# Blockwise causal attention and a max-out MoE layer on one core: transposed q and k copied out of PSUM earlier and in two parts, and the first batch reordered

## The chip, the cores and the metric

The kernel runs on one core of a Trainium2 chip. The metric is the device time in microseconds (us) of one execution. A single execution was also recorded by the hardware profiler; all lines of a profile come from that one.

## The reference

```python
# q, k, v: (8 batches, 8 heads, 576 rows, 64), fp32
scores = q @ k^T / 8
mask   = (row // 64) >= (column // 64)        # causal by blocks of 64
attn   = softmax(where(mask, scores, -1e9))
x      = (attn @ v), heads side by side       # (4608 tokens, 512)
# moe: w1, w2 (512, 1024), w_out (1024, 512)
out    = maximum(x @ w1, x @ w2) @ w_out      # (4608, 512) fp32
```

## The kernel before

Heads are handled in pairs, p = 0 to 31, four pairs to a batch; two pairs with their own q and k loads make a group, g = 0 to 15. The attention of a pair makes transposed scores: keys lie on the partitions, so that exp on ScalarE (ACT) gives a tile aT that TensorE can use as weights against v. The MoE layer works on tokens as they get done. One program order is written by hand for all engines (`manual_schedule`): every engine runs its own instructions in the order of the calls, and waits where a semaphore tells it to.

The steps of one group are these.

- `load_qk` (L111) loads q and k of four heads on the queue of SyncE (SP). With `gated` a small memset on GpSimd (POOL) goes ahead, so that the load starts no earlier than that memset. `load_v` (L131) and `load_w` (L142) load v and the MoE weights from POOL's own queue, and turn them into bf16 on the way.
- `cast` (L125) makes bf16 of q or k, in parts on the engines that it is given.
- `transposes` (L297) transposes q or k of both pairs of a group on TensorE into two PSUM tiles, and returns `copy_out`, which copies them to SBUF (qT, kT): the first by VectorE (DVE), the second mostly by ACT.
- Scores go to PSUM by `burst_p`, `burst_q1`, `burst_q2`, `burst_q3` in batch 0 (L360 to L370) and by `tile_0`, `tile_1`, `tile_2` later (L382 to L399); `exp` (L344) follows on ACT; `mask` (L349) then sets blocks of aT to zero, on POOL unless another engine is named.
- `pad_keys` (L327) copies a little of kT on POOL.
- `av` (L413) multiplies aT by v and normalises on DVE, in two calls for a pair: row tiles 0 and 1 (6 matmuls), then 2, 3 and 4 (24 matmuls). The late one needs all masks of the pair.
- `x_out` (L441) transposes the result to xT, by TensorE and two copies. After the second group of a batch it raises `done_tokens`: 256 after rows 0 to 255 of batch 0, then 576.

MoE matmuls fill TensorE in between. `plan` (L244) makes a list of units: `h_unit(i, f)` is x @ w1 and x @ w2 for a span i of tokens and 128 columns f (8 matmuls), `y_unit` multiplies by w_out. Span 0 is tokens 0 to 255, span 1 tokens 256 to 575, the others have 512 tokens. `fill(n)` (L281) issues steps of that list in order until their cost reaches n, and stops at the first step whose tokens are not done:

```python
    def fill(n):
        while n > 0 and at[0] < len(steps) and steps[at[0]][1] <= done_tokens[0]:
```

A matmul of span 0 costs 0.5, one of 512 tokens costs 1. `fill_of` (L467) gives each group's share of the steps that are ready.

PSUM has two pools: ps_s, two tiles of two banks, for scores; ps_m, four tiles of one bank, for everything else: the transposes, ps_h and ps_y of the MoE layer, ps_o of `av`, the tiles of `x_out`, and those of `warm_up` (L289), which are matmuls on zeros whose result is not used. A tile of ps_m can be taken again when its last reader is done.

Batch 0 (groups 0 and 1) is written out call by call, L501 to L580. The loop at L589 handles groups 2 to 15: scores of a pair, a `fill`, `av` of the pair two before, transposes of the next group (`t_pair`, L496), scores of the next tiles with their exps (`region`, L409), then `copy_out`, then POOL's work (`pool_work`, L474).

Of the kernel before, what the change touches and what calls it, by code (L numbers as in the profile page):

```python
# [9 lines left out]
BF16 = mybir.dt.bfloat16  # L10
# [4 lines left out]
def kernel(  # L15
# [10 lines left out]
    nc = tc.nc  # L26

    B, H, S, D = q.shape
    P = 128
# [6 lines left out]
    NFF = d_ff // P  # L36
# [6 lines left out]
    NP = 64  # L43
    RPP = S // NP
# [9 lines left out]
    NCH = 5  # L54
# [3 lines left out]
    QCUT = 256  # L58
# [14 lines left out]
    NSPAN = len(spans)  # L73
# [3 lines left out]
    tiles = [(carry[i] + w) // P for i, (_, w) in enumerate(spans)]  # L77
# [6 lines left out]
    qkn = ctx.enter_context(tc.tile_pool(name="qkn", bufs=2))  # L84
# [22 lines left out]
    raws = {}  # L107
    qk_n = {}
    dve, pool, act = nc.vector.tensor_copy, nc.gpsimd.tensor_copy, nc.scalar.copy

    def load_qk(g, queues, gated=False):  # L111
        b, u = divmod(g, GPB)
        for nm, src, queue in (("q", q, queues[0]), ("k", k, queues[1])):
            if queue is None:
                continue
            raws[nm, g] = t = raw.tile([P, 2, RPP * D], FP32, name=f"{nm}raw")
            if gated:
                nc.gpsimd.memset(t[:, 0, :1], 0.0)
            queue.dma_start(
                out=t[:],  # L120
                in_=src[b, 4 * u:4 * u + 4].rearrange(
                    "(s h) (p t) d -> (h p) s (t d)", h=2, t=RPP),
            )

    def cast(nm, g, parts):  # L125
        t = raws.pop((nm, g)).rearrange("p s (t d) -> p t s d", d=D)
        qk_n[nm, g] = n = qkn.tile([P, RPP, 2, D], BF16, name=f"{nm}n")
        for copy, j0, j1 in parts:
            copy(out=n[:, j0:j1], in_=t[:, j0:j1])  # L129

# [11 lines left out]
    def load_w(f0, fw, which=(0, 1)):  # L142
        for i in which:
            dst, src = ((w1_sb, w1r), (w2_sb, w2r))[i]
            nc.gpsimd.dma_start(out=dst[:, :, f0:f0 + fw], in_=src[:, :, f0:f0 + fw])
# [11 lines left out]
    nc.vector.memset(zeros[:], 0.0)  # L157
    nc.scalar.activation(out=warm[:], in_=warm[:], func=AF.Exp)
    load_qk(1, (SP, SP))
    load_qk(2, (SP, None))  # L160
    make_identity(nc, ident)
    for r in range(NV):
        nc.vector.memset(vv_r[r][:, :, :, D:D + 1], 1.0)
# [7 lines left out]
    for c in range(2):  # L171
        load_v(0, c)
    load_w(0, 256, (0,))
    cast("k", 1, ((pool, 0, RPP),))
    load_w(0, 256, (1,))
    load_qk(2, (None, SP), gated=True)


    done_tokens = [0]
# [64 lines left out]
    def plan():  # L244
        def h(i, f):
            t0, w = spans[i]
            units.append((h_unit(i, f), t0 + w, w / SPAN, 2 * NDM))

        def y(i, s, last=False):
            t0, w = spans[i]  # L250
            if last:
                units.append((y_last(i, s), t0 + w, 0.333, 3 * NFF))
            else:
                units.append((y_unit(i, s), t0 + w, 1.0, NFF))

        for i in range(NSPAN):
            for f in range(NFF):
                h(i, f)
                if i > 2 and f % 2 == 0 and f // 2 < tiles[i - 1]:
                    y(i - 1, f // 2)  # L260
            if i == 1:
                for j in range(2):
                    for s in range(tiles[j]):
                        y(j, s)
        n = tiles[-1]
        for s in range(n):
            y(NSPAN - 1, s, s == n - 1)
# [13 lines left out]
    def fill(n):  # L281
        while n > 0 and at[0] < len(steps) and steps[at[0]][1] <= done_tokens[0]:
            u, _, cost = steps[at[0]]
            next(u)
            n -= cost
            at[0] += 1


    def warm_up(n):  # L289
        pw = ps_m.tile([P, SPAN], FP32, name="ps_w", tag="m")  # L290
        for _ in range(n):
            nc.tensor.matmul(pw[:], zeros[:, :P], zeros[:], start=True, stop=True)
# [4 lines left out]
    def transposes(nm, g, copies):  # L297
        n = qk_n.pop((nm, g))
        pts = [ps_m.tile([P, RPP, NP], BF16, name=f"ps_{nm}T", tag="m") for _ in range(2)]
        for j in range(RPP):  # L300
            for i in range(2):
                r = slice(i * NP, (i + 1) * NP)
                nc.tensor.transpose(  # L303
                    pts[i][:, j, :], n[r, j].rearrange("p s d -> p (s d)"), ident[r, r],
                )

        def copy_out(which=(0, 1)):
            for i in which:
                t = (qT_r if nm == "q" else kT_r)[(2 * g + i) % NT]
                copies[i](  # L310
                    out=t[:, :S].rearrange("q (p j) -> q p j", j=RPP),
                    in_=pts[i].rearrange("q j p -> q p j"),
                )
        return copy_out

# [44 lines left out]
    def burst_p(p):  # L360
        burst(p, ((0, 0, QCUT), (1, P, QCUT - P)), 0)

    def burst_q1(p):
        burst(p, ((0, QCUT, 320), (1, QCUT, 192)), 384)

    def burst_q2(p):
        burst(p, ((1, 448, P), (2, QCUT, 320), (4, 512, BLK)), 896)
# [4 lines left out]
    def masks_p(p, eng=None):  # L372
        for a in (0, 256):
            mask(p, a, eng)

    def masks_q(p, eng=None):
        for a in (1024, 1408):
            mask(p, a, eng)
# [30 lines left out]
    def region(*tiles):  # L409
        for out in tiles:  # L410
            out()
# [26 lines left out]
            rec[:, :n].to_broadcast([P, n, 2, D]),  # L438
        )

    def x_out(g, t0=0, t1=NCH):  # L441
        b, u = divmod(g, GPB)
        xp = xps[g]
        n = t1 - t0
        n_odd = min(t1, NCH - 1) - t0
        pe = ps_m.tile([P, 2, n, BLK], BF16, name="ps_xe", tag="m")
        po = ps_m.tile([P, 2, n_odd, BLK], BF16, name="ps_xo", tag="m")
        for s in range(2):
            for t in range(t0, t1):
                src = xp[:, t, s].rearrange("p a d -> p (a d)")  # L450
                nc.tensor.transpose(pe[:, s, t - t0, :], src[:BLK], ident[:BLK, :BLK])  # L451
                if t < NCH - 1:
                    nc.tensor.transpose(po[:, s, t - t0, :], src[BLK:], ident[BLK:, BLK:])  # L453
        dst = xT[:, 2 * u:2 * u + 2, b * S + t0 * P:b * S + t1 * P].rearrange(
            "p s (t h w) -> p s t h w", h=2, w=BLK)
        nc.vector.tensor_copy(out=dst[:, :, :, 0], in_=pe[:])  # L456
        nc.vector.tensor_copy(out=dst[:, :, :n_odd, 1], in_=po[:])
        if u == GPB - 1:
            done_tokens[0] = min(b * S + t1 * P, (b + 1) * S)

# [37 lines left out]
        return lambda: [f() for f in outs]  # L498


    warm_up(16)  # L501
    cq = transposes("q", 0, (dve, act))
    ck = transposes("k", 0, (act, dve))
    cq((0,))
    ck((0,))
    cq((1,))
    ck((1,))
    cast("q", 1, ((dve, 0, RPP),))
    burst_p(0)
    masks_p(0)  # L510
    burst_p(1)
    warm_up(2)
    masks_p(1)
    for c in range(2, NCH):
        load_v(0, c)
    load_w(256, 256)
    cq = transposes("q", 1, (dve, dve))
    burst_q1(0)
    ck = transposes("k", 1, (dve, dve))
    for i in range(2):  # L520
        cq((i,))
        ck((i,))
    load_w(512, 512)
    warm_up(3)
    burst_p(2)
    av(0, [0, 1])
    burst_q3(0)
    warm_up(2)
    burst_p(3)
    masks_p(2, nc.vector)  # L530
    av(1, [0, 1])
    masks_p(3, nc.vector)
    burst_q2(0)
    av(2, [0, 1])
    warm_up(2)
    burst_q1(1)
    av(3, [0, 1])
    x_out(0, 0, 2)
    warm_up(2)
    cast("q", 2, ((pool, 0, RPP),))  # L540
    masks_q(0)
    cast("k", 2, ((pool, 0, RPP),))
    burst_q2(1)
    x_out(1, 0, 2)
    warm_up(2)
    burst_q3(1)
    masks_q(1)
    for c in range(3):
        load_v(1, c)
    fill(2)  # L550
    load_qk(3, (SP, SP), gated=True)
    burst_q1(2)
    transposes("q", 2, (dve, act))()
    fill(3)
    burst_q2(2)
    av(0, [2, 3, 4])
# [5 lines left out]
    av(1, [2, 3, 4])  # L562
    fill(2)
    burst_q1(3)
    transposes("k", 2, (dve, act))()
    pad_keys(4)
    pad_keys(5)
    fill(2)
    x_out(0, 2, NCH)
    burst_q2(3)  # L570
    av(2, [2, 3, 4])
    fill(2)
    burst_q3(3)
# [15 lines left out]
    for g in range(GPB, NG):  # L589
        a, b = 2 * g, 2 * g + 1  # L590
        if x_due:
            x_out(x_due.pop())
        n = fill_of(g)
        region(tile_0(a), tile_1(a))
        if g == GPB:
            av(3, [2, 3, 4])
            fill(5)
            x_out(1, 2, NCH)
            n = fill_of(g)
        lo, hi = n // 18, n * 2 // 9  # L600
        for p, tiles in ((a, lambda: (tile_2(a), tile_0(b))), (b, lambda: (tile_1(b), tile_2(b)))):
            fill(hi)
            if g > GPB:
                av_with(p - LAG, lo)
            else:
                fill(lo)
            copy_out = t_pair(p)
            region(*tiles())
            copy_out()
            if p % 2 and g + 1 < NG:  # L610
                pad_keys(p + 1)
                pad_keys(p + 2)
            pool_work(p)
        if g > GPB:
            x_due.append(g - 1)
        fill(n - 2 * (lo + hi))
# [43 lines left out]
```

The softmax here doesn't subtract the row's maximum and nothing guards it: scores larger than these inputs give would overflow.

## Time and profile before

| | us |
|---|---|
| median of 7 runs | 286.73 |
| lowest and highest | 286.25 and 288.73 |
| the profiled execution | 288.19 |
| its span, first to last instruction | 286.3 |
| ACT busy (exps of 128x1024: 92 of 1.02) | 140.9 |
| TensorE: ps_h, 412 matmuls of 128x512 | 102.4 |
| TensorE: ps_y, 273 matmuls | 65.5 |
| first ps_h matmul starts at | 18.23 |

A line of a timeline gives the start, the duration, the engine, the line of the kernel, the operation, out<-in with shapes, and how many instructions are put together; in brackets the engine's idle time just before, and what ended it. PE is TensorE, PEld its weight loads, SPq and POOLq the queues that issue DMAs. The rows of digits cut the span into 40 slices, with the busy share of each in tenths (for DMA, the mean of 16 DMA engines).

### The profile page before, as it was taken

The page shows a single profiled execution, that of the slowest core. Times are in us where ns is not written, and L with a number is a line of the kernel's source. Part 1 is how long each engine was busy: PE and PEld are TensorE (multiplying, and loading weights), DVE is VectorE, ACT ScalarE, POOL GpSimd, SP SyncE. Part 2 cuts the span into 40 slices and gives each one's busy share as a digit, 9 for nine tenths or more (in the row PEclk, how much of TensorE's full clock was granted, in tenths as well). Part 3 has the DMA queues.
Part 4 walks back from the last instruction along what each step waited for, and adds up shares of the span by engine and source line. Part 5 has one row for each costly group of instructions (what it writes and reads, how often), then busy time and mean ns, then how long its engine had stood idle before and what let it go on. Part 6 is the DMA issues. An engine that isn't in the chain of part 4 may idle for free.

```text
span 286.3 us, 7763 instructions
## 1 busy us (share of the span) xinstructions
PE 271.7 (95%) x3207; PEld 152.1 (53%) x3253; DVE 186.6 (65%) x386; ACT 140.9 (49%) x194; POOL 108.8 (38%) x271
## 2 busy tenths in 40 slices
PE   7689999999999999999999999999999999999995
PEld 2346667646555555555546464645555554444443
DVE  4966778758888676666667666667665766455430
ACT  2776486676575557383746646556555100010112
POOL 2987365754744643346253714362211000000000
DMA  7999989968954792669562985266210102011114
GB/s 258 264 208 201 194 200 283 228 86 255 212 35 167 83 231 49 204 71 228 61 205 35 201 93 164 78 76 73 49 39 37 39 37 76 37 64 50 56 54 147
DMA packets 55939, 36.67 MB, mean 128 GB/s; under 512 B 38752, under 2 KB 43232, under 8 KB 55904
## 3 DMA queue, kind: packets, MB, share of 16 engines
q0 software_dynamic: 41728, 7.87, 34.1%
q1 hardware_dynamic: 13760, 27.66, 28.4%
q10 hardware_dynamic: 416, 0.66, 0.7%
q8 instruction: 25, 0.41, 0.6%
q14 instruction: 10, 0.08, 0.1%
HBM read 34.60 MB, written 9.44 MB: 154 GB/s over the span
## 4 chain that ended last, share of the span: by engine, by line
PE 80%; issue 2%; ACT 2%; DVE 1%; ACTq 0%
PE ps_h L197 39%; PE ps_y L215 21%; PE ps_o L429 9%; PE ps_s L321 6%; PE ps_qT L303 2%; PE ps_kT L303 2%; PE ps_xe L451 2%; ACT aT L345 1%; DVE g L206 1%; PE ps_y L231 1%; PE ps_s L339 1%; ACT qT L310 0%; ACT aT L401 0%; ACT kT L310 0%; PE ps_xo L453 0%
## 5 line engine op out<-in xcount | busy, mean ns | idle before, releaser
L197 PE MATMUL ps_h<-xT,w_sb 128*128 128x512 bf16 (+3 forms) x604 | 133.9, 357 | 5.0 <-issue 3.2
L345 ACT ACTIVATE aT<-ps_s 128x1024 bf16<-128x1024 f32 (+2 forms) x100 | 95.9, 993 | 63.6 <-PE ps_s L321 51.8
L197 PEld LDWEIGHTS <-w_sb 128*128 128x128 bf16 x640 | 57.3, 98 | 58.5 <-issue 8.4
L204 DVE CAST h<-ps_h 128x512 bf16<-128x512 f32 (+3 forms) x80 | 51.0, 638 | 29.4 <-PE ps_h L197 27.7
L215 PE MATMUL ps_y<-wo_sb,g 128*128 128x512 bf16 x273 | 65.5, 379 | 0.8 <-issue 0.5
L206 DVE TENSOR_TENSOR g<-h,ps_h 128x512 bf16<-128x512 bf16 (+3 forms) x80 | 50.7, 634 | 11.7 <-PE ps_h L197 9.6
L350 POOL MEMSET aT<- 64x128 bf16 x124 | 22.4, 200 | 91.7 <-ACT aT L345 90.8
L221 ACT COPY y<-ps_y 128x512 f32<-128x512 f32 x31 | 18.3, 591 | 71.4 <-PE ps_y L215 56.7
L429 PEld LDWEIGHTS <-aT 128*128 128x128 bf16 x960 | 37.1, 98 | 15.7 <-issue 4.5
L215 PEld LDWEIGHTS <-g 128*128 128x128 bf16 x280 | 27.0, 98 | 32.1 <-issue 1.1
L429 PE MATMUL ps_o<-vv,aT 128*128 128x65 bf16 x960 | 40.2, 194 | 1.0 <-DMA vv<-in_v_dram 0.4
L133 POOL DMA_DIRECT2D vv<-in_v_dram x40 | 33.7, 847 | 0.5
L436 DVE TENSOR_TENSOR xp<-ps_o,rec 128x256 bf16<-128x256 f32 (+1 forms) x64 | 31.4, 491 | 2.2
L321 PE MATMUL ps_s<-qT,kT 64*128 64x64 bf16 (+6 forms) x344 | 31.8, 279 | 1.1 <-ACT kT L310 0.7
L435 DVE RECIPROCAL rec<-ps_o 128x4 f32<-128x4 f32 (+1 forms) x64 | 12.0, 187 | 24.5 <-PE ps_o L429 22.9
L129 POOL CAST qn<-qraw 128x1152 bf16<-128x1152 f32 (+1 forms) x15 | 16.5, 1100 | 8.8 <-DMA qraw<-in_q_dram 8.7
L187 POOL COPY g<-g 128x512 bf16<-128x512 bf16 x8 | 4.9, 614 | 38.5 <-DVE g L206 38.4
L129 POOL CAST kn<-kraw 128x1152 bf16<-128x1152 f32 x15 | 17.3, 1154 | 5.7 <-DMA kraw<-in_k_dram 5.7
L456 DVE COPY xT<-ps_xe 128x640 bf16<-128x640 bf16 (+2 forms) x18 | 8.2, 453 | 15.6 <-PE ps_xe L451 14.9
L321 PEld LDWEIGHTS <-kT 64*128 64x128 bf16 x344 | 13.7, 95 | 6.3 <-issue 2.8
L310 DVE COPY qT<-ps_qT 128x576 bf16<-128x576 bf16 x17 | 12.7, 749 | 0.7 <-PE ps_qT L303 0.7
L310 DVE COPY kT<-ps_kT 128x576 bf16<-128x576 bf16 x17 | 12.7, 749 | 0.4 <-PE ps_kT L303 0.4
(44 smaller groups left out, 141.6 us busy)
## 6 DMA issues: line engine op xcount, KB each, us to landing
qraw<-in_q_dram SPq DMA_DIRECT2D x16, 576.0 KB, 4.2
out_dram<-y SPq DMA_DIRECT2D x35, 256.0 KB, 2.6
kraw<-in_k_dram SPq DMA_DIRECT2D x15, 576.0 KB, 5.9
vv<-in_v_dram POOLq DMA_DIRECT2D x32, 128.0 KB, 5.3
w_sb<-in_moe_w_dram POOLq DMA_DIRECT2D x4, 256.0 KB, 8.7
w_sb<-in_moe_w_dram POOLq DMA_DIRECT2D x2, 512.0 KB, 12.5
wo_sb<-in_moe_w_out_dram POOLq DMA_DIRECT2D x2, 512.0 KB, 12.5
kraw<-in_k_dram ACTq DMA_DIRECT2D x1, 576.0 KB, 5.9
```

Of the source, the lines that this page charges most:

```text
L129: copy(out=n[:, j0:j1], in_=t[:, j0:j1])
L133: nc.gpsimd.dma_start(out=vv_r[b % NV][P - rows:, c, :, :D], in_=v[b, :, c * P:c * P + rows, :].rearrange("h p d -> p h d"),)
L197: nc.tensor.matmul(pt[:, :w], w_sb[:, c, f * P:(f + 1) * P], xT[:, c, t0:t0 + w], start=(c == 0), stop=(c == NDM - 1),)
L204: nc.vector.tensor_copy(out=h1[:, :w], in_=pt[:, :w])
L206: nc.vector.tensor_max(g[:, f, m:m + w], h1[:, :w], pt[:, :w])
L215: nc.tensor.matmul(py[:], g[:, f, s * P:(s + 1) * P], wo_sb[:, f, :], start=(f == 0), stop=(f == NFF - 1),)
L310: copies[i](out=t[:, :S].rearrange("q (p j) -> q p j", j=RPP), in_=pts[i].rearrange("q j p -> q p j"),)
L321: nc.tensor.matmul(ps[:, hh, col:col + w], kT[r, k0:k0 + P], qT[r, q0:q0 + w], start=True, stop=True,)
L345: nc.scalar.activation(out=aT_r[p % NA][:, :, a0:a0 + w], in_=ps[:, :, :w], func=AF.Exp, scale=scale,)
L350: (eng or nc.gpsimd).memset(aT_r[p % NA][BLK:, :, a0:a0 + BLK], 0.0)
L429: nc.tensor.matmul(po[:, gi, hh, :], a[:, hh, a0:a0 + P], vv[:, c, h0 + 2 * hh, :], start=(mm == 0), stop=(mm == n_mm - 1),)
L436: nc.vector.tensor_mul(xp[:, ts[0]:ts[0] + n, :, p % 2], po[:, :, :, :D], rec[:, :n].to_broadcast([P, n, 2, D]),)
```

## The change

The change has two parts.

The first is in the loop of groups 2 to 15 and touches every group: `copy_out()` is called ahead of `region(...)`, so the copies of qT or kT stand ahead of the exps in ACT's queue; and `lo`, the cost of MoE matmuls between the two `av` calls of a pair, is at least 3.

The second is batch 0. `copy_out` can copy a part of the columns, LOW (columns 0 to 260) or HIGH (261 to 575), and on a named engine. The copies of groups 0 and 1 are made in these parts. The casts of group 1 are shared by DVE and POOL. q and k of group 2 are both loaded later, gated behind the v loads of batch 0. All first halves of `av` and both `x_out` of rows 0 to 255 come before most of the bursts q1, q2 and q3; x_out of group 0 is copied by ACT. There are fewer warm-up matmuls (24 in place of 29). The transposes of group 2 come later, and `plan` orders the units of spans 0 and 1 by halves of f: f 0 to 3 of span 0, then of span 1, then f 4 to 7 of both.

```diff
     def cast(nm, g, parts):
-        t = raws.pop((nm, g)).rearrange("p s (t d) -> p t s d", d=D)
-        qk_n[nm, g] = n = qkn.tile([P, RPP, 2, D], BF16, name=f"{nm}n")
+        t = raws[nm, g].rearrange("p s (t d) -> p t s d", d=D)
+        if (nm, g) not in qk_n:
+            qk_n[nm, g] = qkn.tile([P, RPP, 2, D], BF16, name=f"{nm}n")
+        n = qk_n[nm, g]
...
     load_qk(1, (SP, SP))
-    load_qk(2, (SP, None))
...
     load_w(0, 256, (0,))
-    cast("k", 1, ((pool, 0, RPP),))
+    cast("q", 1, ((pool, 6, RPP),))
+    cast("k", 1, ((pool, 4, RPP),))
     load_w(0, 256, (1,))
-    load_qk(2, (None, SP), gated=True)
...
-        for i in range(NSPAN):
-            for f in range(NFF):
+        for f0 in (0, NFF // 2):
+            for i in range(2):
+                for f in range(f0, f0 + NFF // 2):
+                    h(i, f)
+        for i in range(1, NSPAN):
+            for f in range(NFF if i > 1 else 0):
                 h(i, f)
...
-        def copy_out(which=(0, 1)):
+        def copy_out(which=(0, 1), part=(0, NP), copy=None):
+            p0, p1 = part
             for i in which:
                 t = (qT_r if nm == "q" else kT_r)[(2 * g + i) % NT]
-                copies[i](
-                    out=t[:, :S].rearrange("q (p j) -> q p j", j=RPP),
-                    in_=pts[i].rearrange("q j p -> q p j"),
+                (copy or copies[i])(
+                    out=t[:, p0 * RPP:p1 * RPP].rearrange("q (p j) -> q p j", j=RPP),
+                    in_=pts[i][:, :, p0:p1].rearrange("q j p -> q p j"),
...
-    def x_out(g, t0=0, t1=NCH):
+    def x_out(g, t0=0, t1=NCH, copies=(dve, dve)):
...
+    LOW = (0, -(-QCUT // RPP))
+    HIGH = (LOW[1], NP)
     warm_up(16)
     cq = transposes("q", 0, (dve, act))
     ck = transposes("k", 0, (act, dve))
-    cq((0,))
-    ck((0,))
-    cq((1,))
-    ck((1,))
-    cast("q", 1, ((dve, 0, RPP),))
+    cq((0,), LOW)
+    ck((0,), LOW)
+    ck((1,), LOW)
+    cq((1,), LOW)
+    cq((0,), HIGH)
+    cast("q", 1, ((dve, 0, 6),))
+    cast("k", 1, ((dve, 0, 4),))
     burst_p(0)
     masks_p(0)
+    cq((1,), HIGH)
+    ck((0,), HIGH)
     burst_p(1)
+    ck((1,), HIGH)
     warm_up(2)
     masks_p(1)
+    load_w(256, 256)
     for c in range(2, NCH):
         load_v(0, c)
-    load_w(256, 256)
-    cq = transposes("q", 1, (dve, dve))
...
+    load_qk(2, (SP, SP), gated=True)
+    load_w(512, 512)
+    cq = transposes("q", 1, (dve, act))
+    ck = transposes("k", 1, (dve, dve))
+    cq((0,), LOW)
+    cq((1,), LOW)
+    ck((0,), LOW)
+    ck((1,), LOW)
+    cq((0,), HIGH, act)
+    cq((1,), HIGH, dve)
+    warm_up(2)
+    burst_p(2)
+    ck((0,), HIGH, act)
+    av(0, [0, 1])
+    masks_p(2, nc.vector)
+    burst_p(3)
+    av(1, [0, 1])
+    ck((1,), HIGH, act)
+    masks_p(3, nc.vector)
+    warm_up(1)
+    av(2, [0, 1])
+    x_out(0, 0, 2, (act, act))
+    warm_up(1)
+    av(3, [0, 1])
     burst_q1(0)
...
+    warm_up(1)
+    x_out(1, 0, 2, (dve, dve))
+    burst_q2(0)
+    warm_up(1)
+    fill(2)
     burst_q3(0)
...
+    masks_q(0)
     burst_q1(1)
...
+    fill(1)
     burst_q2(1)
...
+    fill(1)
     burst_q3(1)
     masks_q(1)
+    cast("q", 2, ((pool, 0, RPP),))
+    cast("k", 2, ((pool, 0, RPP),))
     for c in range(3):
         load_v(1, c)
     fill(2)
     load_qk(3, (SP, SP), gated=True)
     burst_q1(2)
-    transposes("q", 2, (dve, act))()
...
     burst_q1(3)
+    transposes("q", 2, (dve, act))()
+    fill(2)
+    x_out(0, 2, NCH)
+    burst_q2(3)
     transposes("k", 2, (dve, act))()
     pad_keys(4)
     pad_keys(5)
-    fill(2)
-    x_out(0, 2, NCH)
-    burst_q2(3)
     av(2, [2, 3, 4])
...
-        lo, hi = n // 18, n * 2 // 9
+        lo, hi = max(3, n // 18), n * 2 // 9
...
             copy_out = t_pair(p)
-            region(*tiles())
+            outs = tiles()
             copy_out()
+            region(*outs)
```

In the lines before, batch 0 ran its bursts q1, q3, q2 of pair 0 and q1 of pair 1 among the AVs of pairs 0 to 3, with `warm_up` calls of 2 and 3 between them.

More of the change, by code (lines that the diff above doesn't have):

```diff
@@ L455, in x_out @@
             "p s (t h w) -> p s t h w", h=2, w=BLK)
-        nc.vector.tensor_copy(out=dst[:, :, :, 0], in_=pe[:])
-        nc.vector.tensor_copy(out=dst[:, :, :n_odd, 1], in_=po[:])
+        copies[0](out=dst[:, :, :, 0], in_=pe[:])
+        copies[1](out=dst[:, :, :n_odd, 1], in_=po[:])
         if u == GPB - 1:
@@ L503 @@
     ck = transposes("k", 0, (act, dve))
-    cq((0,))
-    ck((0,))
-    cq((1,))
-    ck((1,))
-    cast("q", 1, ((dve, 0, RPP),))
+    cq((0,), LOW)
[5 more added lines that the diff above has]
+    cast("k", 1, ((dve, 0, 4),))
     burst_p(0)
     masks_p(0)
+    cq((1,), HIGH)
+    ck((0,), HIGH)
     burst_p(1)
+    ck((1,), HIGH)
     warm_up(2)
     masks_p(1)
+    load_w(256, 256)
     for c in range(2, NCH):
         load_v(0, c)
-    load_w(256, 256)
-    cq = transposes("q", 1, (dve, dve))
-    burst_q1(0)
[L519 to L526, printed above, removed]
-    burst_q3(0)
[L528 to L535, printed above, removed]
-    burst_q1(1)
[L537 to L542, printed above, removed]
+    load_qk(2, (SP, SP), gated=True)
[22 more added lines that the diff above has]
+    av(3, [0, 1])
+    burst_q1(0)
+    warm_up(1)
[3 more added lines that the diff above has]
+    fill(2)
+    burst_q3(0)
+    masks_q(0)
+    burst_q1(1)
+    fill(1)
     burst_q2(1)
-    x_out(1, 0, 2)
-    warm_up(2)
+    fill(1)
     burst_q3(1)
     masks_q(1)
+    cast("q", 2, ((pool, 0, RPP),))
+    cast("k", 2, ((pool, 0, RPP),))
     for c in range(3):
```

## The prediction

> **What bounds the kernel now.** I read the page's parts 1, 2 and 4, then the windows by stage, then each engine's timeline where TensorE isn't full.
>
> ```profile
> PE 271.7 (95%) x3207; PEld 152.1 (53%) x3253; DVE 186.6 (65%) x386; ACT 140.9 (49%) x194; POOL 108.8 (38%) x271
> PE   7689999999999999999999999999999999999995
> DMA  7999989968954792669562985266210102011114
> PE 80%; issue 2%; ACT 2%; DVE 1%; ACTq 0%
> ```
>
> TensorE is the bound: 95% busy and 80% of the chain. Only the first slices (7.2 us each) leave room, and there the DMA engines are full too. Work on TensorE isn't changed, warm-ups apart, so the end moves by what TensorE idles less or more. Two places matter.
>
> First, from 38 us to 210 us, TensorE waits a little for PSUM buffers which the copies of qT and kT still hold:
>
> ```profile
> 122.83 1.02 ACT L345 ACTIVATE aT<-ps_s 128x1024 bf16<-128x1024 f32 x1
> 123.75 0.63 ACT L310 COPY qT<-ps_qT 128x576 bf16<-128x576 bf16 x1
> ...
> 123.86 0.59 PE L197 MATMUL ps_h<-xT,w_sb 128*128 128x512 bf16 x2
> 124.43 0.65 PE L429 MATMUL ps_o<-vv,aT 128*128 128x65 bf16 x16
> ...
> 58.18 0.42 PE L303 MATMUL ps_kT<-ident,kn 64*128 64x64 bf16 x17 [0.40 <-ACT qT L310]
> ```
>
> The two ps_h matmuls issue 0.216 us apart, so ps_o could start at 124.29; it starts at 124.43, right after ACT's copy ends (123.75 + 0.63 = 124.38). That copy stood behind two exps.
>
> Second, batch 0. What sets its pace is GpSimd's queue and the loads:
>
> ```profile
> 11.62 0.37 SPq L119 DMA_DIRECT2D kraw<-in_k_dram  x1
> 24.26 0.37 SPq L119 DMA_DIRECT2D qraw<-in_q_dram  x1
> 24.67 0.47 SPq L119 DMA_DIRECT2D kraw<-in_k_dram  x1
> ...
> 19.95 1.15 POOL L129 CAST kn<-kraw 128x1152 bf16<-128x1152 f32 x1 [0.71 <-DMA kraw<-in_k_dram]
> 21.45 2.64 POOL L133 DMA_DIRECT2D vv<-in_v_dram  x3
> 24.33 0.34 POOL L350 MEMSET aT<- 64x128 bf16 x2
> 24.62 1.56 POOL L133 DMA_DIRECT2D vv<-in_v_dram  x2
> 31.43 1.15 POOL L129 CAST qn<-qraw 128x1152 bf16<-128x1152 f32 x1 [2.52 <-DMA qraw<-in_q_dram]
> 34.76 1.15 POOL L129 CAST kn<-kraw 128x1152 bf16<-128x1152 f32 x1 [2.18 <-DMA kraw<-in_k_dram]
> ...
> 22.18 0.78 PE L429 MATMUL ps_o<-vv,aT 128*128 128x65 bf16 x15 [0.44 <-DMA vv<-in_v_dram]
> 29.36 0.92 PE L429 MATMUL ps_o<-vv,aT 128*128 128x65 bf16 x24
> 31.98 1.48 PE L197 MATMUL ps_h<-xT,w_sb 128*128 128x256 bf16 x12
> ```
>
> A cast that ends its wait on a load shows the landing: k of group 2 took 8.3 us (11.62 to 19.95), q and k of group 3 7.2 and 10.1 us (24.26 to 31.43, 24.67 to 34.76). The v loads of batch 1 and the masks of pair 2 (24.33) stand behind the cast of k2. The late AV of pair 3 (29.36) comes 0.45 us after its masks end (28.71 + 0.20).
>
> **What the Trainium skill says.** "PSUM — Partial Sum Buffer", section "Engine vs sequencer instructions": the queues of ScalarE, VectorE and GpSimdE are strict FIFO. The trace agrees: the copy at 123.75 waits out the exps although its transposes were done at 121. "DMA: Bandwidth & Descriptors", section "Queues, rings and completion order": each DMA engine takes turns between the queues packet by packet, so a q load shares the engines with v and weights. The trace fits: 7.2 and 10.1 us to landing above, against 3.7 us at the fastest (listing of line 119). "TensorE: Matmul & The Clock Gate", Part 1: after an idle window of about 3.4 us the array runs at half clock. Before, the clock stays at 1.00 in every window; my gaps below stay under 2 us, so I cost this at nothing.
>
> **Part 1: copies ahead of the exps, and `lo` at least 3.** No instruction is added. ACT's copy moves before two exps; ACT is idle there (2.58 us until the exp at 121.48), so the exps end as late as before. Waits of TensorE that such copies end: 0.14 in each of the eight groups from 94 to 200 us (1.1), 0.40 at 58.18, about 0.3 each at 47.27 and 39.94: 2.1 us. Next late would be VectorE's release of a ps_h buffer; at 124.43 that had ended at 122.91. `lo` of 3 puts one more matmul (0.216 us) between two AV groups; five AV starts between 64 and 90 us wait 0.2 to 0.3 us for VectorE, 1.3 us together, and may lose all or none. Gain 0.8 to 3.2 us; I take 1.5, since a removed wait here often meets the next in a queue of four buffers.
>
> **Part 2: batch 0, edit by edit.** Copies: a 576-column copy (DVE 0.75, ACT 0.64) becomes 261 + 315 columns. From the ACT rows (128x384 exp 0.49, 128x1024 1.02: 0.83 ns a column, 0.16 fixed) the halves cost 0.37 + 0.42; on DVE about 0.42 + 0.48. The first exp can start at 9.0 instead of 9.29. But ACT now also has four HIGH copies before and between the exps of pairs 0 to 3 (1.7 us) and x_out(0)'s two copies (0.7). Group 1's casts: DVE 1280 columns (0.90 + 0.60) instead of 1152 (1.34), GpSimd 1024 (0.5 + 0.7) instead of 1152 (1.15): transposes of k1 0.2 us earlier at most, since they wait for the HIGH copies to free PSUM (10.5). Warm-ups: 24 instead of 29 matmuls, all in gaps: nothing.
>
> Followed along the queues: exps of pairs 2 and 3 at 12.9 and 14.0 (before 12.98 and 14.45), x_out(1) at 16.7, first ps_h at 17.6 (18.23 before): 0.6 earlier. The price is that the exps of q1 and q2 of pair 0 and q1 of pair 1, done by 17.2 before, now begin at 16.4. Then ACT runs on end: q1 of pair 2 at 20.9 (19.20 before), q1 of pair 3 at about 25.8.
>
> Loads: q2 and k2 leave at 15.8 (after w(256), v of batch 0 and two gate memsets on POOL) instead of 2.26 and 11.62. v of batch 0 is issued at 13.2 instead of 12.22, behind two more weight loads on POOL; it needed until 22.18 before, now 22.5 to 23.5. At 7.2 and about 9 us, q2 lands at 23 and k2 at 25 (23 to 26.5).
>
> POOL then, in order: cast k2 to 26.15, v(1) x3 to 28.75, gates 0.15, masks of pair 2 to 29.2, v(1) x2 to 30.8, pad_keys (0.3 each) to 31.4, masks of pair 3 to 31.8. Behind them on TensorE: late AV of pair 2 at 29.2 (before 26.61), of pair 3 at 31.85 (29.36). Then 0.85 us of AV, 0.8 of reciprocal and multiply, x_out, 0.7 of copies: ps_h resumes at 34.6, where 31.98 stood.
>
> Filler: the new order lets only f 0 to 3 of span 0 run before x_out(1): 4 units x 8 x 0.5 = 16 of cost. fill calls up to AV of pair 2 ask for 16, so fill(3) and fill(5) after it are empty, where the old order used 20. That is 8 matmuls x 0.109 = 0.87 us done later. Loss: 34.6 - 31.98 + 0.87 = 3.5 us, less 0.4 for the wait on the k3 cast at 35.97, which the later TensorE no longer meets: 3.1 us. A wait for a weight load (0.24 at 31.16, w of f 4) is inside the 31.98.
>
> **Sum.** +3.1 - 1.5 = +1.6 us. The profiled execution took 288.19 us with a span of 286.3, 1.9 outside it, and lies above the median of 286.73; I add the difference to the median: 288.3.
>
> **Rivals.**
> 1. The loads are not late (ends faster). Two loads less at the start; if k2 lands within 6.5 us of issue (by 22.5), its cast hides behind ACT's backlog, masks of pair 2 are done at 26.7, AV of pair 3 at 30.0, ps_h at 32.8 at the latest and 31.8 if v comes by 22. Loss 0.9; with the 2.3 of part 1: 285.3. For it: 3.7 us is the fastest landing. Against: both neighbours in that stretch took 7 us and more, with DMA at 9 tenths. It decides at k2's landing.
> 2. Both cancel: k2 at 24, part 1 at 2.2: +2.3 - 2.2, 286.8.
> 3. Batch 0 worse: ACT, with 2.4 us more in front of it, and v of batch 0 after 24 push one another, k2 at 26.5: ps_h at 36.5, loss 5, gain 1.5: 290.2.
> That the copies don't go ahead can't be: the calls are in that order on every queue.
>
> **Chances.** Forecast 0.43, rival 3 0.13, rival 2 0.26, rival 1 0.18. Half a per cent, 1.43 us, is what a measurement here can tell. Slower 0.55 (forecast's lower edge goes to "same"), within 0.27, faster 0.18. Range: rival 1 to a little beyond rival 3, 285.2 to 290.8; the forecast's own is 287.4 to 289.4.
>
> **What would show it.** Part 1: no gap before ps_o after qT copies, 58.18's wait gone. Part 2: k2's cast at 24 to 26 on POOL; masks of pairs 2 and 3 at 29 and 32; ps_o of pair 3 released by POOL; TensorE slices 4 and 5 emptier. Wrong if k2 is cast by 22.5, if ps_h runs on between 30 and 33, or if TensorE's clock falls below 1.00.

## The result: slower, and the profile after

| | before | changed |
|---|---|---|
| median of all runs, us | 286.93 (31 runs) | 291.00 (12 runs) |
| lowest and highest | 286.14 and 291.32 | 288.63 and 293.85 |
| the profiled execution, its span | 288.19, 286.3 | 291.21, 289.4 |
| `x_out(1, 2, NCH)`, the last of batch 0, starts on TensorE | 31.70 | 37.76 |
| first ps_y matmul | 50.97 | 56.91 |

Changed over before is 1.0119, with a 95% interval of 1.0096 to 1.0143: 3.4 us slower by the ratio, 4.1 by the medians.

The page of the changed kernel, parts 1, 2 and 4:

```profile
PE 272.4 (94%) x3205; PEld 153.0 (53%) x3248; DVE 184.4 (64%) x387; ACT 141.9 (49%) x202; POOL 108.2 (37%) x273
PE   8796689999999999999999999999999999999995
PEclk9999599999999999999999999999999999999999
DMA  7999979997993398529853893566211102011114
PE 86%; DMA 6%; POOL 5%; issue 2%; DVE 1%; ACT 0%; SPq 0%; POOLq 0%
```

In the second row TensorE's fourth and fifth slices (21.7 to 36.2 us) fell from 9 and 9 tenths to 6 and 6, and the granted clock (PEclk, in tenths of full speed) shows a 5 in the fifth. DMA and POOL have come into the chain, together 11%. From the seventh slice on the row is as full as before: the loss arises before 43 us.

SP's queue and GpSimd's timeline of the changed kernel:

```profile
15.79 0.37 SPq L119 DMA_DIRECT2D qraw<-in_q_dram  x1
16.20 0.98 SPq L119 DMA_DIRECT2D kraw<-in_k_dram  x1
```

```profile
24.80 1.14 POOL L131 CAST qn<-qraw 128x1152 bf16<-128x1152 f32 x1 [4.16 <-PE ps_h L198]
27.83 1.15 POOL L131 CAST kn<-kraw 128x1152 bf16<-128x1152 f32 x1 [1.88 <-DMA kraw<-in_k_dram]
28.92 2.63 POOL L135 DMA_DIRECT2D vv<-in_v_dram  x3
...
31.75 0.34 POOL L357 MEMSET aT<- 64x128 bf16 x2
...
34.23 0.20 POOL L357 MEMSET aT<- 64x128 bf16 x1
35.12 0.20 POOL L357 MEMSET aT<- 64x128 bf16 x1 [0.69 <-ACT aT L352]
```

The loads left when predicted, 15.8 and 16.2, and took 9.0 and 11.6 us until their casts could start. The releaser shown at 24.80, a ps_h matmul, can't be what a cast of q waits for; I put that wait down to the load. The masks of pair 2 (31.75) stand behind the cast of k and three v loads. TensorE in the same stretch, and its windows (columns: PE busy, count; PEld; DVE; ACT; POOL; clock; DMA share; GB/s):

```profile
26.00 0.44 PE L309 MATMUL ps_qT<-ident,qn 64*128 64x64 bf16 x18 [0.87 <-POOL qn L131]
...
29.03 0.44 PE L309 MATMUL ps_kT<-ident,kn 64*128 64x64 bf16 x18 [1.21 <-POOL kn L131]
29.40 0.23 PE L436 MATMUL ps_o<-vv,aT 128*128 128x65 bf16 x2
32.01 1.40 PE L436 MATMUL ps_o<-vv,aT 128*128 128x65 bf16 x22 [2.37 <-POOL aT L357]
33.21 1.04 PE L198 MATMUL ps_h<-xT,w_sb 128*128 128x256 bf16 x4
...
35.66 1.22 PE L436 MATMUL ps_o<-vv,aT 128*128 128x65 bf16 x24
38.04 0.45 PE L198 MATMUL ps_h<-xT,w_sb 128*128 128x320 bf16 x2
```

```profile
25.00:30.00 5.00, 2.39 (x62) 1.47 (x58) 2.66 (x7) 3.15 (x4) 3.12 (x4) 0.96 1.00 182
30.00:35.00 5.00, 2.95 (x30) 1.93 (x31) 1.44 (x4) 0.60 (x2) 4.27 (x11) 0.50 1.37 110
35.00:40.00 5.00, 3.74 (x50) 2.57 (x50) 1.98 (x6) 2.00 (x3) 1.35 (x2) 0.86 1.17 242
```

Three waits on GpSimd, 0.87 + 1.21 + 2.37 = 4.45 us, all go back to the two late loads: with early loads, below, none of the three is left. From 29.6 to 36.4 us the clock is at half: 22 AV matmuls take 1.40 us, where 24 took 0.92, and four of ps_h 1.04 in place of 0.60.

### The profile page after: what moved, and what is told of

Read it like the earlier page. It is cut to its first block, busy times and chain, and to the rows that moved or that the text cites. A ratio compares the mean times of both kernels' runs of the same rounds, so it can differ in the third digit from the quotient of the medians.

```text
span 289.4 us, 7767 instructions
## 1 busy us (share of the span) xinstructions
PE 272.4 (94%) x3205; PEld 153.0 (53%) x3248; DVE 184.4 (64%) x387; ACT 141.9 (49%) x202; POOL 108.2 (37%) x273
## 4 chain that ended last, share of the span: by engine, by line
PE 86%; DMA 6%; POOL 5%; issue 2%; DVE 1%; ACT 0%; SPq 0%; POOLq 0%
PE ps_h L198 42%; PE ps_y L216 21%; PE ps_o L436 10%; PE ps_s L328 6%; DMA kraw<-in_k_dram 4%; POOL vv L135 2%; DMA qraw<-in_q_dram 2%; PE ps_qT L309 2%; PE ps_kT L309 2%; PE ps_xe L458 2%; POOL w_sb L147 1%; POOL kn L131 1%; PE ps_y L232 1%; PE ps_s L346 1%; POOL qn L131 0%
## 5 line engine op out<-in xcount | busy, mean ns | idle before, releaser
L198 PE MATMUL ps_h<-xT,w_sb 128*128 128x512 bf16 (+3 forms) x605 | 137.0, 358 | 1.9 <-issue 0.3
L198 PEld LDWEIGHTS <-w_sb 128*128 128x128 bf16 x640 | 57.9, 98 | 58.4 <-issue 9.1
L436 PEld LDWEIGHTS <-aT 128*128 128x128 bf16 x960 | 38.3, 99 | 16.9 <-POOL aT L357 2.5
L436 PE MATMUL ps_o<-vv,aT 128*128 128x65 bf16 x960 | 41.2, 195 | 2.9 <-POOL aT L357 2.4
L317 ACT COPY qT<-ps_qT 128x576 bf16<-128x576 bf16 (+2 forms) x18 | 10.5, 590 | 31.2 <-PE ps_qT L309 31.2
L131 POOL CAST qn<-qraw 128x1152 bf16<-128x1152 f32 (+2 forms) x16 | 17.2, 1078 | 11.6 <-DMA qraw<-in_q_dram 4.5
L131 POOL CAST kn<-kraw 128x1152 bf16<-128x1152 f32 (+1 forms) x15 | 17.0, 1136 | 6.4 <-DMA kraw<-in_k_dram 4.7
L317 ACT COPY kT<-ps_kT 128x576 bf16<-128x576 bf16 (+2 forms) x18 | 10.6, 590 | 15.9 <-PE ps_kT L309 15.8
L463 DVE COPY xT<-ps_xe 128x640 bf16<-128x640 bf16 (+2 forms) x17 | 7.9, 463 | 16.2 <-PE ps_xe L458 15.4
## 6 DMA issues: line engine op xcount, KB each, us to landing
wo_sb<-in_moe_w_out_dram POOLq DMA_DIRECT2D x2, 512.0 KB, 11.7
```

The lines of the kernel that those rows point to most:

```text
L198: nc.tensor.matmul(pt[:, :w], w_sb[:, c, f * P:(f + 1) * P], xT[:, c, t0:t0 + w], start=(c == 0), stop=(c == NDM - 1),)
L317: (copy or copies[i])(out=t[:, p0 * RPP:p1 * RPP].rearrange("q (p j) -> q p j", j=RPP), in_=pts[i][:, :, p0:p1].rearrange("q j p -> q p j"),)
L436: nc.tensor.matmul(po[:, gi, hh, :], a[:, hh, a0:a0 + P], vv[:, c, h0 + 2 * hh, :], start=(mm == 0), stop=(mm == n_mm - 1),)
```

## The experiments

Each of them gives the median of its own runs, with the ratio to the kernel before, measured on the same chip (medians there 286.7 to 287.1). Intervals are some 0.2% wide to each side, and a step between two kernels has the width of both, so steps under about 0.8 us are not told apart. Differences are of medians; where the ratios give a clearly different figure, it stands beside them.

### Part 1 by itself

The kernel before, with the copies ahead and `lo` of 3; then with the copies alone, without the line of `lo`.

```diff
-        lo, hi = n // 18, n * 2 // 9
+        lo, hi = max(3, n // 18), n * 2 // 9
...
-            region(*tiles())
+            outs = tiles()
             copy_out()
+            region(*outs)
```

> The kernel before with the first part alone: copies ahead of the exps, and lo at least 3. Theory now (the lag of 7.7 us at the first MoE matmuls of span 1 shrinks to 2.9 at the end, so the first part gains 4 to 4.7 us): 282.5 to 283.5 us. Rival (my forecast: waits meet the next one in the queue, 1.5 us): 285.4. If the shrinking lag is an effect of batch 0 having been late (MoE work left over fills gaps later), it shows no more than 1.5 us here too.

> The kernel before with the copies ahead of the exps alone, lo as before. Both together gain 4.15 us. Theory (waits held by ScalarE's copies go, 2.1 us; waits for VectorE in groups 4 to 7 stay, they are lo's part): 284.5 to 285.2. Rival (copies do it all, earlier release of two of four PSUM buffers changes every group): 283.

Measured: 282.70 us, 0.9868 [0.9846, 0.9889], and for the copies alone 284.21, 0.9900 [0.9872, 0.9929]. Part 1 gains 4.2 us (3.8 by the ratio), of which 2.8 come from the copies; the other 1.5 (0.9 by the ratios) go to `lo`, which is at the edge of what can be told. Part 1 alone is faster than both kernels, and nothing that was tried beats it. Its page, parts 1 and 2, and its TensorE timeline in the loop:

```profile
PE 274.3 (98%) x3253; PEld 151.5 (54%) x3253; DVE 185.5 (66%) x386; ACT 139.5 (50%) x194; POOL 107.7 (38%) x271
PE   8799999999999999999999999999999999999995
```

```profile
112.61 2.33 PE L197 MATMUL ps_h<-xT,w_sb 128*128 128x512 bf16 x10
114.78 0.34 PE L429 MATMUL ps_o<-vv,aT 128*128 128x65 bf16 x6
```

Ten matmuls 0.216 us apart end at 114.77, and ps_o starts at 114.78: the 0.14 us that the prediction showed before ps_o is gone, here and in every group. The changed kernel has the same copies and the same `lo`; if they gain as much there, its second part costs not 4 but 291.0 - 282.7 = 8.3 us (7.2 by the ratios).

### The loads of q and k of group 2

First the changed kernel with these loads as before; then the other way round, part 1 alone with the loads moved late.

```diff
 load_qk(1, (SP, SP))
+    load_qk(2, (SP, None))
...
     load_w(0, 256, (1,))
+    load_qk(2, (None, SP), gated=True)
...
-    load_qk(2, (SP, SP), gated=True)
```

> The changed kernel with the q and k loads of group 2 put back to their early places, all else as changed. Theory (late q2 and k2 hold up GpSimd's queue, and through it the late AVs of pairs 2 and 3): the whole loss of batch 0 goes, k2 is cast by 21, x_out of group 1 comes before 33 us instead of at 37.8, and the gain of the later groups stays: 282 to 284 us, faster than before. Rival (the reordering itself costs batch 0: copies in ACT's queue, the order by halves of f, empty fills): at most half comes back, 288 us or more.

> The kernel before with part 1 alone (282.7 us) and the loads of q and k of group 2 moved as the change moves them: both gated behind the v loads of batch 0 and the weights w(256). If late loads cost the same in the old order as in the new one (291.0 against 286.3): 287.0 to 287.8. If the old order has more slack for them than the new one, since its TensorE has other work then: 284 to 286. If the late loads only hurt together with the new order: 282.4 to 283.4.

Measured: 286.32, 0.9979 [0.9960, 0.9998]: 4.7 us come back (4.0 by the ratios), about the three waits above. In the old order late loads cost more, 289.89, 1.0106 [1.0066, 1.0146], which is 7.2 above 282.70 (6.8 by the ratios). GpSimd's timeline of the first, TensorE's of the second:

```profile
21.09 1.14 POOL L131 CAST qn<-qraw 128x1152 bf16<-128x1152 f32 x1
22.17 1.15 POOL L131 CAST kn<-kraw 128x1152 bf16<-128x1152 f32 x1
...
26.10 0.34 POOL L359 MEMSET aT<- 64x128 bf16 x2
```

```profile
17.91 0.39 PE L319 MATMUL ps_s<-qT,kT 64*128 64x320 bf16 x4
25.27 0.66 PE L301 MATMUL ps_qT<-ident,qn 64*128 64x64 bf16 x18 [6.97 <-POOL qn L129]
```

One wait of 6.97 us is about the whole loss. In the old order the transposes of q of group 2 come early on TensorE and stop it outright; the change puts them later, which takes some of the cost off but not all. With the early loads the casts no longer wait (no bracket), and the masks of pair 2 come 5.65 us sooner.

### The masks behind those casts

The masks of pairs 2 and 3 on DVE; then also the gate of group 3's loads ahead of the casts.

```diff
-    masks_q(2)
+    masks_q(2, nc.vector)
...
-    masks_q(3)
+    masks_q(3, nc.vector)
```

> The changed kernel with the four masks of pairs 2 and 3 (bursts q2, q3) set by VectorE instead of GpSimd; the loads stay late. Theory (the masks stand behind the k2 cast and three v issues on GpSimd): the late AV of pair 2 starts right after the transposes of k2 at 29.1 instead of 32.0, that of pair 3 near 31.5 instead of 35.7; the clock stays full; 3 to 4.5 us come back: 286 to 288 us. Rival (late data, not the queue, sets the pace): the transposes of k2 still wait until 29 and less than 1.5 us come back: 289.5 or more.

> The changed kernel with the masks of pairs 2 and 3 on VectorE as in e2, and the gates of the q and k loads of group 3 moved ahead of the casts of group 2 on GpSimd. In e2 x_out of group 1 came 3.5 us earlier, but then the transposes of q3 waited 2.5 us for their cast, since that load too was issued behind GpSimd's queue. Theory (one queue delays load after load): q3 is cast by 35, that wait goes, 287 to 288.5 us. Rival (the load engines are full, an earlier issue lands no earlier, and takes from q2 and k2): 290 or more.

Measured: 290.78, 1.0136 [1.0095, 1.0177], no gain that can be told. TensorE's timeline of the first:

```profile
30.00 0.90 PE L436 MATMUL ps_o<-vv,aT 128*128 128x65 bf16 x24
...
32.43 0.91 PE L436 MATMUL ps_o<-vv,aT 128*128 128x65 bf16 x24
...
39.46 0.44 PE L309 MATMUL ps_qT<-ident,qn 64*128 64x64 bf16 x18 [2.32 <-POOL qn L131]
```

The AVs come 2.0 and 3.2 us sooner, and TensorE then meets the cast of group 3's q, whose load had been gated behind the same casts. The second run took that wait away as well (these transposes then start at 37.34 with no wait), but its four executions took 287.30, 288.20, 292.24 and 293.13 us, without an interval: inconclusive.

### The clock

More warm-ups where the clock had fallen: 8 matmuls ahead of the late AV of pair 2 (the first edit of the diff), 3 and 4 more about that of pair 3. Then 8 more before 20 us (its second edit is one of three), in a kernel with early loads and v of batch 0 ahead of the weights, which follows below.

```diff
+    warm_up(8)
     av(2, [2, 3, 4])
...
-    warm_up(2)
+    warm_up(5)
     burst_p(2)
```

> The changed kernel with 8 warm-up matmuls ahead of the late AV of pair 2, 3 ahead of that of pair 3 and 4 after it, where TensorE waits anyway. Theory A (the half clock between 30 and 36 us is a cost of its own): the clock stays at 1.00, AVs and scores run at full speed, 0.8 to 1.5 us come back: 289.5 to 290.2. Theory B (the masks on GpSimd alone set the times, what runs in between has slack): within 0.5 us of the changed kernel, 291.

> The changed kernel with q and k of group 2 loaded as before and v of batch 0 ahead of the weights (285.7 in its own run), and with 8 more warm-up matmuls before 20 us: 5 instead of 2 after the exps of pair 1, 5 instead of 2 before burst_p of pair 2, 3 instead of 1 before av of pair 2. Theory A, the half-speed stretch of TensorE (15 to 20 us in that kernel, clock 0.51) is what the new order of batch 0 still costs: the clock is 1.00 in every window and the time falls by 1.5 to 2.5 us, to 283.2 to 284.2. Theory B, the order of the bursts costs it, through queues on ACT and TensorE: the time stays within 0.6 of 285.7 whatever the clock does. Theory C, warm-ups in front of the AVs delay them: slower by up to 1 us.

Measured: 291.01, 1.0148 [1.0110, 1.0185], and 285.75, 0.9959 [0.9940, 0.9978]. Windows of the first run; then of the kernel with v ahead, and of the same with the 8 warm-ups:

```profile
10.00:15.00 5.00, 3.90 (x59) 2.09 (x52) 3.55 (x12) 3.23 (x8) 4.96 (x11) 0.63 1.30 145
15.00:20.00 5.00, 4.77 (x53) 2.22 (x50) 2.55 (x10) 3.51 (x8) 2.29 (x7) 0.69 1.58 152
```

```profile
10.00:15.00 5.00, 3.56 (x62) 2.21 (x62) 3.60 (x12) 3.65 (x8) 4.94 (x12) 0.80 1.66 209
15.00:20.00 5.00, 4.94 (x47) 2.19 (x46) 2.13 (x9) 2.93 (x5) 2.32 (x4) 0.51 1.99 200
```

```profile
10.00:15.00 5.00, 3.41 (x61) 1.97 (x63) 3.08 (x11) 2.69 (x6) 4.94 (x11) 1.00 1.67 207
15.00:20.00 5.00, 4.63 (x62) 2.30 (x61) 2.80 (x11) 4.38 (x8) 2.24 (x5) 1.00 1.85 200
```

In the first run the half-clock stretch only went elsewhere (0.63 and 0.69 from 10 to 20 us); one of its executions kept a mean clock of 1.000 and took 291.70. In the second the stretch is gone, and the time is the same, 285.75 against 285.70. So the clock isn't what is left of the loss there. What it costs in the changed kernel isn't shown: of its 12 executions nine have a mean clock of 0.988 or less and took 288.98 to 293.85, two have 0.999 or more and took 288.96 and 290.97. Elsewhere a lower clock does go with a longer time, as the runs with the bursts put back show below.

### What is left: 3.6 us of the new order

With early loads the changed kernel is still 286.32 - 282.70 = 3.6 us behind part 1 alone (3.2 by the ratios). The first rows are edits on the changed kernel, one after the other: a row with a plus keeps the edits above it. The last two rows start from part 1 alone, and add the split copies of group 0 and the shared casts of group 1.

| kernel | us | ratio to before |
|---|---|---|
| early loads (above) | 286.32 | 0.9979 [0.9960, 0.9998] |
| + v of batch 0 ahead of w(256) | 285.70 | 0.9957 [0.9939, 0.9974] |
| + 8 warm-ups (above) | 285.75 | 0.9959 [0.9940, 0.9978] |
| + casts of group 2 ahead of the masks, as before | 285.46 | 0.9947 [0.9929, 0.9965] |
| + old order of f | 284.71 | 0.9921 [0.9894, 0.9947] |
| old order of calls, copies and casts in parts | 282.91 | 0.9857 [0.9836, 0.9878] |
| same, new order of f | 283.16 | 0.9867 [0.9842, 0.9893] |

The edits on v, on GpSimd's order and on the units; the last one backwards makes the last row of the table:

```diff
-    load_w(256, 256)
     for c in range(2, NCH):
         load_v(0, c)
+    load_w(256, 256)
...
+    cast("q", 2, ((pool, 0, RPP),))
     masks_q(0)
+    cast("k", 2, ((pool, 0, RPP),))
...
-        for f0 in (0, NFF // 2):
-            for i in range(2):
...
+        for i in range(NSPAN):
+            for f in range(NFF):
```

> Early loads as in e1, and v of batch 0 issued ahead of the second weight load again, as before the change. Theory (TensorE's waits for v in the late AV of pair 0, 0.54 and 0.36 us in e1, are part of what e1 still loses): those waits go, 285.3 to 285.9 us. Rival (TensorE then waits for the exps instead, which are late anyway): 286.3, unchanged.

> The kernel of 285.75 us with early loads, v of batch 0 ahead and 8 more warm-ups, whose clock stays at 1.00, and in it the casts of q and k of group 2 on GpSimd as before the change: q ahead of the masks of pair 0, k behind them, instead of both behind the masks of pair 1. Theory D, what is left of the loss is GpSimd's order: its casts wait behind masks that wait on exps (2.17 and 1.81 us idle), and v of batch 1, the gate of group 3's loads and the masks of pairs 2 and 3 wait behind the casts: group 3's loads leave about 4 us earlier, q of group 3 is cast near 30 instead of 33.5, and the time falls by 1.5 to 2.5, to 283.2 to 284.2. Theory E, the exps that were moved behind the first AVs hold TensorE back whatever GpSimd does: within 0.6 of 285.75, the late AV of pair 0 still at 23.1.

> The kernel of 285.46 us (early loads, v of batch 0 ahead, 8 more warm-ups, casts of group 2 ahead on GpSimd) with the units of spans 0 and 1 in the old order, so that all eight f of span 0 may run before x_out(1). Theory F, what is left of the loss is filler: in that kernel the fills around the AV of pair 3 are empty, and TensorE idles 0.65 + 1.05 + 0.43 us between 29 and 34 us where the old order idles 0.5: 283.2 to 284.2 and the waits after the AV of pair 3 filled with ps_h. Theory E, the exps behind the first AVs: within 0.6 of 285.46, since the wait only moves to the first weights or to v.

> The first part, plus of the second part only the copies of group 0 in LOW and HIGH columns and the shared casts of group 1; bursts, AVs, loads and fills in the order of before. e1 still loses 3.6 us to the first part alone. Theory (the new order of batch 0 costs it: eight exps stand in one row on ScalarE, from 15.6 to 22.6 us, because AVs and x_out were put ahead of their bursts): here the loss is absent, 282.2 to 283.2 us. Rival (the split copies and casts cost it, by two more fixed starts per tile and HIGH copies ahead of exps): 285 or more.

> The kernel of 282.91 us (part 1, split copies and shared casts, old order of batch 0) with the new order of units in spans 0 and 1: 4 units of span 0, worth 16, are all that may run before x_out(1), where the old order of calls asks for 20 and more. Theory F: the fills of 3 and 5 ahead of x_out(1) are cut short, TensorE idles there, 1.3 to 2.2 us slower, 284.2 to 285.1. If the order of f costs nothing: 282.6 to 283.3.

Splitting the copies and sharing the casts costs nothing that can be told (282.91 against 282.70). No single step of the first five rows is told apart from nothing; the four steps together, 1.6 us, are. The order of f makes 0.75 in the new order of calls and 0.25 in the old; the timelines show what it does. TensorE with the new order of f, then with the old:

```profile
30.49 0.91 PE L438 MATMUL ps_o<-vv,aT 128*128 128x65 bf16 x24
32.28 0.20 PE L460 MATMUL ps_xe<-ident,xp 64*128 64x64 bf16 x1 [0.88 <-DVE xp L445]
...
32.56 0.45 PE L200 MATMUL ps_h<-xT,w_sb 128*128 128x320 bf16 x2
```

```profile
30.99 0.91 PE L433 MATMUL ps_o<-vv,aT 128*128 128x65 bf16 x24
31.74 1.26 PE L200 MATMUL ps_h<-xT,w_sb 128*128 128x256 bf16 x10
```

Above, the fill behind the AV of pair 3 is empty, and TensorE waits 0.88 us for DVE to normalise; below, ten ps_h matmuls stand there. Some 1.8 us, from 284.71 to 282.91, stay without a cause. The traces of these two kernels say where they arise: the late AV of pair 0 starts at 23.31 against 20.20, and ps_h resumes after the last x_out of batch 0 at 33.44 against 30.62, so the lag has arisen by the first late AV. Putting the bursts back among the AVs was tried twice, with v ahead and with the casts ahead:

```diff
     cq = transposes("q", 1, (dve, act))
+    burst_q1(0)
...
     av(0, [0, 1])
+    burst_q3(0)
...
     masks_p(3, nc.vector)
+    burst_q2(0)
...
+    burst_q1(1)
     av(3, [0, 1])
```

> The same kernel of 285.7 us, with burst_q1, q3, q2 of pair 0 and burst_q1 of pair 1 put back among the AVs of pairs 0 to 3, as in the kernel before; warm-ups, split copies, shared casts, x_out on ACT and the order of f stay as changed. Theory B, the order of the bursts costs what is left: 282.7 to 283.7. Theory A, the clock and the fewer warm-ups do: the denser work of TensorE before 15 us may keep the clock at 1.00, then the two theories give the same time and the clock by windows says which; if the clock still falls and the time is under 284, the clock isn't the cost; if the clock still falls and the time stays at 285 or more, the clock is the cost.

> The same, and also the bursts q1, q3, q2 of pair 0 and q1 of pair 1 back among the AVs. If D is the whole cause: the same as the run with the casts alone. If it takes both, since the masks that the casts waited on come from those exps: the casts alone give under 1 us and this one 282.7 to 283.5. If neither is the cause: 285 or more, and the split copies of group 1, x_out on ScalarE and the place of group 2's transposes are what is left.

Measured: 286.14, 0.9975 [0.9953, 0.9996], and 287.55, 1.0014 [0.9997, 1.0030]: no gain, and in the second a loss of 2.1. Half of that loss goes with the clock: five executions with a mean clock of 0.999 or more took 286.34 to 286.61, nine with 0.994 took 287.48 to 287.84, 1.2 us more in the median, while all six of the kernel with the casts alone had 0.998 or more. In the first, nine executions with 0.999 or more have a median of 285.49, seven with 0.981 or 0.982 one of 287.77. So at full clock the first gains nothing either, and the second loses 1.0. That the clock makes the difference, and not what lowers it, is not shown. In the profiled execution of the second, at 0.994, the first ps_h matmul starts at 21.12, where it started at 18.34 with the casts alone: TensorE is later before the MoE work begins. Which of the remaining moves costs the 1.8 (the order of the bursts, x_out on ACT, group 1's copies in parts, the later transposes of group 2, or several together) stays open: the bursts were put back only in the new order of f, and the others were not tried by themselves.

### Single edits on the way

The changed kernel with the old order of f; the same with early loads; and the changed kernel with the 512-column weights later:

```diff
     load_qk(2, (SP, SP), gated=True)
-    load_w(512, 512)
...
     load_qk(3, (SP, SP), gated=True)
+    load_w(512, 512)
```

> The changed kernel with the old order of the units of spans 0 and 1, loads still late. Theory (the late loads hold x_out of group 1, whatever TensorE does meanwhile; more MoE work then fits into the waits): x_out of group 1 stays near 37.5 us, 0.9 to 2 us come back: 289 to 290. Rival (order of f is neutral): 291.

> Early loads of group 2 as in e1, and the MoE units of spans 0 and 1 back in the old order (all eight f of span 0 first), the rest as changed. e1 is still 3.6 us slower than the first part alone. Theory (the empty fills: after 32 matmuls of span 0 nothing is ready, so TensorE stands idle before x_out of group 1, 0.65 + 1.05 + 0.43 us in e1): 284 to 285 us. Rival (the batch-0 exps come late on ScalarE, 20 to 27 us, and v of batch 0 behind the weights): no more than 0.5 us back, 286.

> The changed kernel with the last weight load (columns 512 to 1023 of w1 and w2) moved behind the v loads of batch 1 and the gates of group 3, so that it no longer shares the DMA engines with q2 and k2. Theory (q2 and k2 are late because they share with 4 MB of weights and v): k2 is cast by 24 instead of 27.8, the masks of pair 2 are set by 28, x_out of group 1 comes by 34: 287 to 289.5, if the weights are in time for f 4. Rival (landing is late from the issue at 15.8 on, whatever shares): k2 after 26, 290.5 or more.

Measured: 291.18, 1.0136 [1.0111, 1.0161]; 285.91, 0.9964 [0.9942, 0.9985]; 289.62, 1.0085 [1.0054, 1.0116]. With late loads the order of f makes no difference that can be told. Without the 512-column weights in their way q and k of group 2 are cast at 23.99 and 25.45, 0.8 and 2.4 us sooner, but TensorE waited for v of batch 0 until 25.35, and only 1.4 us (1.0 by the ratios) came of it.

## Why the prediction failed: the direction held, two sizes didn't

It said 288.3 and slower, for late loads that hold up GpSimd and through its masks the AVs; the runs show that mechanism (late loads alone: 4.7 to 7.2 us). The time lies 2.7 above it. Two terms of the sum were mis-sized in opposite directions: the loss of part 2 by 5.2, the gain of part 1 by 2.7. That the miss is no larger is the luck of two errors that cancel in part.

- **Part 1, "I take 1.5, since a removed wait here often meets the next".** Measured 4.2 (3.8 by the ratio), above its upper bound of 3.2. The list of waits (2.1 held by ACT, 1.3 by DVE) was most of the gain, measured as 2.8 and 1.5. TensorE is 98% busy with part 1 alone: no other wait of that size took their place. The discount had no line of the profile behind it.
- **Part 2, 3.1.** Measured 8.3 (7.2 by the ratios). Its terms:
  - *Landing, "at 7.2 and about 9 us, q2 lands at 23 and k2 at 25".* Measured 9.0 and 11.6: the cast of k at 27.83, 2.8 later than the prediction, and the masks of pair 2 at 31.75, 2.55 later than its 29.2. This failed step is the largest. The 7.2 was that of q of group 3, and k of that group had taken 10.1 already. Those two were issued at 24.3 beside five v loads of 128 KB; here four weight loads and three of v, 1.9 MB by part 6 of the page, were issued from 11.7 to 17.2. Without the two 512-column weight loads q and k took 8.4 and 9.4 (15.62 to 23.99, 16.04 to 25.45), so these loads explain a part of it.
  - *The start of the sum, "34.6 - 31.98".* That 31.98 came from one execution 1.5 above the median. The same code of batch 0 resumes ps_h at 30.31 with the copies alone and 30.48 with part 1. The line below, of the kernel before, has a wait on a weight load that the copies-alone profile lacks: the lateness sat inside the stretch that was compared. The loss was counted from that late point and then added to the median, which made it about 1.5 too small.

```profile
20.21 0.83 PE L197 MATMUL ps_h<-xT,w_sb 128*128 128x256 bf16 x6 [0.78 <-DMA w_sb<-in_moe_w_dram]
```

  - *The clock, "I cost this at nothing".* It fell to half for 6.8 us, from 29.6 to 36.4. A clock below 1.00 was named as a sign of being wrong, and came; what it cost in this kernel is not shown.
  - *Together, at "ps_h resumes at 34.6".* It resumed at 38.04, 3.4 later; 2.55 of that stood in the masks of pair 2 already, and the rest came up to 38.04, most of the time at half clock. With the 1.5 of the start point that is 4.9 of the 5.2 that were missing. These are readings of single executions, so the agreement is no proof.
- **Empty fills, 0.87.** In the changed kernel itself the old order of f gave nothing (291.18 against 291.00): the late loads leave TensorE waiting anyway. With early loads it gave 0.4 to 0.75, below what is told apart.
- **Rival 1, decided "at k2's landing".** With the early loads k2 is cast at 22.17, inside its bound of 22.5. The loss of part 2 was then 3.6, where the rival had 0.9: the new order has costs that the prediction didn't follow.
- **Rival 3, "ps_h at 36.5, loss 5", 290.2.** It came nearest, with k2 cast even later than its 26.5. Its other half, "v of batch 0 after 24", did not happen: the last wait for v ended at 22.78.
- **Right:** issue at 15.8, v of batch 0 waited for until 22.78, the first exp at 8.55 (said 9.0), masks of pairs 2 and 3 behind k2's cast, late AV of pair 2 released by POOL, no gap before ps_o in the loop, TensorE's slices 4 and 5 emptier.

## What to carry to other kernels

Before a load is moved later, find the first instruction that waits for what it brings, and all that stands behind that one in its queue: here masks, v loads and the gate of the next group stood behind one cast, and taking the masks alone off it only uncovered the next wait. Price a landing by transfers issued into the same load, not by the neighbours that are at hand, and take the start point of a sum from more than one execution, or from the same one as the total. Test the parts of a change alone: one of these was worth 4 us and hid behind the other.

## What the runs showed of the hardware

The clock fell to half without a long idle stretch. The Trainium skill, "TensorE: Matmul & The Clock Gate", Part 1, gives an idle window of about 3.4 us; a wait of 6.97 us did bring it down (0.70 and 0.62 in the windows from 20 to 30 us of part 1 with late loads, so at about 22.0, 3.7 us into the wait). But in the changed kernel the windows put the fall at about 29.6 us ((1 - 0.96) x 5 / 0.5 = 0.4 us before 30), when the 2.37 us wait had hardly begun and the longest one behind it was 1.21 us; TensorE was busy for 2.39 of the 5 us from 25 to 30. The kernel with v ahead is a second case: (1 - 0.80) x 5 / 0.5 = 2.0 us before 15, so at about 13.0, its clock fell with no wait of TensorE above 0.63 us in the 3.4 us before. Here the measurement decides: partial idleness was enough. How much of it is needed isn't shown: in the 3.4 us from 9.6 to 13.0 that kernel's TensorE was busy for 2.12 us, and that of the kernel with 8 more warm-ups, which kept a clock of 1.00, for 1.92. The time at half is about a multiple of 3.4 us: mean clocks of 0.994, 0.988 and 0.982 over spans near 286 us come again and again, and (1 - 0.994) x 286 / 0.5 = 3.4, with 6.9 and 10.3 for the other two; this fits the window length that the page gives.
